# One adaLN transformer block on one core: an exp issued ahead of later softmaxes, one block's statistics on VectorE, the last rows in 384 and 128 columns, another issue order

## The chip, the core and the metric

The kernel runs on one core of a Trainium2 chip. The core has five engines that run side by side: TensorE (matmuls; PE in the profile, its weight loads PEld), VectorE (DVE), ScalarE (ACT), GpSimd (POOL) and SyncE (SP), which here only issues DMAs. Each engine works through its own list in the order in which the program issued it, and waits on semaphores for the others. The metric is the device time of one execution in microseconds (us); the median of several runs counts.

## The reference

```python
x = A_x                                                       # (1, 2048, 512), bfloat16
mod = (silu(c) @ w_mod).reshape(1, 6, 1, 512)                 # sa, ca, ga, sb, cb, gb
h = layernorm(x) * (1 + ca) + sa
x = x + ga * attention(h, wqkv, wo)
h = layernorm(x) * (1 + cb) + sb
x = x + gb * ((gelu(h @ w_gate) * (h @ w_up)) @ w_down)       # hidden width 1792
# attention: 32 heads of 16; position s attends to s, s-2, ..., s-14 (8 places):
#   softmax over the 8 logits q[s].k[s-2w] / 4, those before position 0 masked out
```

## The kernel before, in words

**Tiling.** The 2048 rows are worked in four groups of 512 rows (sg = 0 to 3), each of four blocks of 128 rows (c4 = 0 to 3). For each group the stages are: norm 1 (`ln1`, `norm`), transpose so that features lie on partitions (`transp`, `transp_ev`), the q, k and v projections (`qkv`, evicted by `qkv_ev`), logits, softmax, weighted sum, output projection (`x1_mm`) with the residual added (`x1_ev`, line 744), norm 2, the two up projections (`ffn_mm`, line 763), gelu and product (`ffn_act`, lines 796 and 803; `ffn_dve`, line 814), and the down projection (line 775) with the residual (line 821) and a store of each block of 128 rows (line 846).

**Attention without small matmuls.** VectorE multiplies q with the eight shifted views of k (`logits`, line 616, one instruction of 128x4096 for each of four slices j), and TensorE adds up each head's 16 products with a matrix of ones and zeros, 32 rows at a time, four at once (`logits_mm`, line 630, tile LTp in PSUM). The softmax (`soft`) takes the maximum (line 647), subtracts it (653), takes exp on ScalarE (658), sums (663), inverts (669) and scales (674). The weights go out to DRAM and come back spread over partitions (`pt_dma`: lines 681 and 688, tile PT). v goes out too and comes back as four loads (`vload`: 590 and 598, tile V). VectorE multiplies them (`pv`, line 700), and TensorE adds up over the eight places with the same ones (line 714, tile o_ps).

**Norms.** `norm` takes the statistics of a block on VectorE (line 394, then the aggregate in 400 and an added constant in 414); the blocks listed in the table `ACT_CH` get theirs on ScalarE, by a Copy and a Square pass that add up their output (`norm_act`, lines 377 and 383; the constant in 419). GpSimd raises to the power of -1/2 (line 425, tile rstd) for all four blocks of a group at once. VectorE then norms the blocks (line 434, tile xn). Group 3's norm 1 is transposed by a DMA (line 454), and ScalarE scales and shifts the result in place (line 486, tile hT).

**Table loads.** ScalarE works exp and gelu from different tables; where the next function needs the other one, the program has an ACT_TABLE_LOAD just ahead of the instruction. At the start the program issues a tiny exp into a scratch tile (line 325), so that exp's table is there early; for groups 2 and 3, whose softmax comes between gelus, there is none.

**What sets the order.** Every stage is a generator of operations (`Op`: an engine, a function that issues one or a few instructions, what must have been issued before, which slots of a pool it takes and gives back). `Issuer.run` goes through the table `ORDER`: each number says from which generator the next operation is taken. Since each engine runs in issue order, this table of 869 numbers is the schedule. The pools are small: four PSUM banks for the large matmuls (tag mm), two for attention (att), one pair for the logits (lg), four product tiles (prod), three each for gelu outputs and casts.

**DMAs.** All loads and stores but two go through SP's queue, in order; a DMA that waits for a semaphore holds up those behind it.

**The last rows.** The last block of group 3 is computed in two halves of 256 columns (line 786), each evicted (828) and stored (837) by itself.

Of the kernel before, what the change touches and what calls it, by code (L numbers as in the profile page):

```python
# [8 lines left out]
ACT = mybir.ActivationFunctionType  # L9
ALU = mybir.AluOpType  # L10
# [94 lines left out]
def kernel(  # L105
# [13 lines left out]
    nc = tc.nc  # L119
# [243 lines left out]
    ACT_CH = {"LN1.0": (3, 4), "LN1.1": (3, 4), "LN1.2": (2, 4), "LN1.3": (0, 4), "LN2.0": (0, 2), "LN2.1": (0, 4)}  # L363
# [274 lines left out]
    def soft(sg):  # L638
# [20 lines left out]
        yield Op("ACT", 0.97, f, after=[f"z.{sg}"], act="exp", fire=f"e.{sg}")  # L659
# [17 lines left out]
        yield Op("DVE", 1.14, f, give=[SL["lg"]], fire=f"p.{sg}")  # L677

# [75 lines left out]

    def ffn_mm(sg):
# [24 lines left out]
        if sg == NSG - 1:  # L780
            for ch in range(2):
                def f(ch=ch):
                    ps = T("mm", [P, D // 2], F32, "y_ps")
                    B["yl", ch] = ps
                    for ft in range(FT):
                        nc.tensor.matmul(ps[:], lhsT=B["hh", sg, ft][:, (CPS - 1) * P:],  # L786
                                         rhs=B["Wd", ft // 4][:, ft % 4, ch * 256:ch * 256 + 256],
                                         start=(ft == 0), stop=(ft == FT - 1))
                yield Op("PE", 1.53, f, take=[SL["mm"]], fire=f"yl.{ch}")
# [19 lines left out]
    def ffn_dve(sg):  # L809
# [13 lines left out]
        if sg == NSG - 1:  # L823
            for ch in range(2):
                def f(ch=ch):
                    ot = T("o", [P, D // 2], BF16, "ot")
                    B["otl", ch] = ot
                    nc.vector.tensor_tensor(out=ot[:], in0=B["yl", ch][:],
                                            in1=B["x", sg][:, CPS - 1, ch * 256:ch * 256 + 256], op=ALU.add)
                yield Op("DVE", 0.37, f, after=[f"yl.{ch}"], take=[SL["o"]], give=[SL["mm"]], fire=f"otl.{ch}")  # L830

    def stores(sg):
        if sg == NSG - 1:
            yield from stores_n(sg, CPS - 1)
            for ch in range(2):
                def f(ch=ch):
                    nc.sync.dma_start(out=out[0, S - P:S, ch * 256:ch * 256 + 256], in_=B["otl", ch][:])
                yield Op("SP", 0.4, f, after=[f"otl.{ch}"], give=[SL["o"]], fire=f"sto.l{ch}", lat=0.15)
# [20 lines left out]
    for sg in range(NSG):  # L859
        for n, g in (("sa1", lambda q: norm_act(lambda: B["x", q], x_ready(q), f"LN1.{q}")),  # L860
# [4 lines left out]
            pl.spawn(g(sg))  # L865
    with tc.manual_schedule():
        pl.run()
# [30 lines left out]
```

## Time and profile before

| | us |
|---|---|
| three runs | 237.60, 237.67, 239.79 |
| median | 237.67 |
| the profiled execution, its own time | 237.65 |
| its span, first to last instruction | 235.9 |
| TensorE busy | 230.1 (98%) |
| VectorE busy | 167.0 (71%) |
| ScalarE busy | 150.1 (64%) |
| GpSimd busy | 29.2 (12%) |
| granted TensorE clock | 1.000 |

In the lines of the timeline the columns are: start (us from the span's start), duration, engine, source line, operation, output tile<-inputs, shapes, count of merged instructions, and in brackets the idle time of the engine before it with what ended it. SPq is SP's queue, issuing a DMA. Lines of groups give busy time and mean ns of one after the bar, lines of DMA issues the KB of one and the median us from issue to landing.

### The profile page before, as it was taken

How to read it: one execution, taken by the hardware profiler on the slowest of the kernel's cores; microseconds unless marked ns; L12 is line 12 of the kernel's file. 1: busy time of each engine (PE TensorE's matmuls, PEld its weight loads, DVE VectorE, ACT ScalarE, POOL GpSimd, SP SyncE). 2: the span in 40 equal slices, each digit the busy share in tenths (PEclk: the TensorE clock that was granted, in tenths of full speed). 3: DMA queues.
4: the chain of work that ended last, by engine and by line, in shares of the span. 5: the costliest groups of instructions: out<-in, count | busy, mean ns of one | idle time of the engine just before them, and what ended most of it. 6: DMA issues, size and time to landing. Idle time of an engine off the chain costs nothing.

```text
span 235.9 us, 3647 instructions
## 1 busy us (share of the span) xinstructions
PE 230.1 (98%) x1382; PEld 107.7 (46%) x1382; DVE 167.0 (71%) x237; ACT 150.1 (64%) x284; POOL 29.2 (12%) x37
## 2 busy tenths in 40 slices
PE   7999999999999999999999999999999999999994
PEld 2755454434544444444443444444444444444444
DVE  4889998999998999969999988937622030423222
ACT  4899998696996758648556772652578531366400
POOL 3215205793100000200000010000100000000000
PEclk9999999999999999999999999999999999999999
DMA  6998775899667076052202833201040000100011
GB/s 218 385 306 272 260 235 149 195 382 408 279 186 195 0 250 253 0 114 74 61 0 61 307 90 69 67 0 44 22 92 1 0 22 0 47 0 22 0 44 47
DMA packets 30217, 30.42 MB, mean 129 GB/s; under 512 B 14712, under 2 KB 26104, under 8 KB 30200
## 3 DMA queue, kind: packets, MB, share of 16 engines
q1 hardware_dynamic: 29664, 29.67, 39.8%
q10 hardware_dynamic: 536, 0.53, 0.6%
q8 instruction: 11, 0.18, 0.3%
q14 instruction: 6, 0.05, 0.1%
HBM read 22.78 MB, written 5.31 MB: 119 GB/s over the span
## 4 chain that ended last, share of the span: by engine, by line
PE 75%; DVE 13%; DMA 4%; ACT 4%; issue 1%; POOL 1%; SPq 0%; ACTq 0%
PE u_ps L763 18%; PE g_ps L763 18%; PE y_ps L775 14%; PE qkv_ps L553 11%; PE x_ps L735 6%; DVE pq L616 5%; PE LTp L630 3%; PE o_ps L714 3%; DMA wm<-in_w_mod_dram 2%; DMA hT<-xn 2%; PE y_ps L786 1%; ACT hT L486 1%; DVE ssum L663 1%; DVE pv L700 1%; DVE e L674 1%
## 5 line engine op out<-in xcount | busy, mean ns | idle before, releaser
L763 PE MATMUL g_ps<-h,Wg 128*128 128x512 bf16 x224 | 57.2, 379 | 0.1
L763 PE MATMUL u_ps<-h,Wu 128*128 128x512 bf16 x224 | 57.2, 379 | 0.0
L814 DVE TENSOR_TENSOR hht<-gl,ub 128x512 bf16<-128x512 bf16 x56 | 22.9, 419 | 40.7 <-ACT ub L803 31.6
L796 ACT ACTIVATE gl<-g_ps 128x512 bf16<-128x512 f32 x56 | 33.6, 600 | 27.5 <-PE g_ps L763 25.9
L775 PE MATMUL y_ps<-Wd,hht 128*128 128x512 bf16 x210 | 47.0, 379 | 0.0
L803 ACT CAST ub<-u_ps 128x512 bf16<-128x512 f32 x56 | 32.8, 586 | 16.7 <-PE u_ps L763 16.5
L553 PE MATMUL qkv_ps<-hT,wqkv 128*128 128x512 bf16 x184 | 42.2, 380 | 0.2 <-ACT hT L486 0.2
L616 DVE TENSOR_TENSOR pq<-qT,kT 128x4096 bf16<-128x4096 bf16 x16 | 36.1, 2284 | 0.8 <-ACT kT L569 0.8
L700 DVE TENSOR_TENSOR pv<-PT,V 128x4096 bf16<-128x4096 bf16 x16 | 35.9, 2282 | 0.0
L763 PEld LDWEIGHTS <-Wg 128*128 128x128 bf16 x224 | 21.8, 98 | 27.1 <-issue 1.1
L763 PEld LDWEIGHTS <-Wu 128*128 128x128 bf16 x224 | 21.6, 98 | 27.2 <-issue 1.7
L775 PEld LDWEIGHTS <-hht 128*128 128x128 bf16 x210 | 20.4, 98 | 25.2 <-issue 0.8
L553 PEld LDWEIGHTS <-wqkv 128*128 128x128 bf16 x184 | 20.3, 114 | 18.8 <-issue 2.3
L425 POOL TENSOR_TENSOR rstd<-rstd,neghalf 128x4 f32<-128x4 f32 (+1 forms) x9 | 10.1, 1123 | 129.7 <-DVE rstd L414 70.0
L586 POOL COPY vh<-vT 128x64 bf16<-128x64 bf16 x3 | 15.9, 5284 | 7.9 <-ACT vT L571 7.9
L821 DVE TENSOR_TENSOR ot<-y_ps,x 128x512 bf16<-128x512 f32 x15 | 10.2, 685 | 7.5 <-PE y_ps L775 7.5
L735 PE MATMUL x_ps<-woP,oT 128*128 128x512 bf16 x64 | 15.5, 379 | 0.0
L744 DVE TENSOR_TENSOR x<-x_ps,x 128x512 bf16<-128x512 f32 x16 | 10.6, 682 | 5.4 <-PE x_ps L735 5.1
L394 DVE BATCH_NORM_STATS2 st<-x 128x6 f32<-128x512 bf16 x18 | 11.8, 680 | 2.5 <-DMA x<-in_A_x_dram 2.5
L377 ACT ACTIVATE gl<-x 128x512 bf16<-128x512 bf16 x14 | 9.1, 649 | 6.2 <-DVE x L744 4.5
L486 ACT ACTIVATE h<-h,modT,scl 128x512 bf16<-128x512 bf16 x12 | 9.0, 804 | 6.3 <-DMA h<-xn 6.3
L725 ACT CAST oT<-o_ps 128x512 bf16<-128x512 f32 x16 | 8.9, 583 | 4.5 <-PE o_ps L714 4.5
(76 smaller groups left out, 188.9 us busy)
## 6 DMA issues: line engine op xcount, KB each, us to landing
V<-vscr SPq DMA_DIRECT2D x16, 526.0 KB, 6.4
wm<-in_w_mod_dram SPq DMA_DIRECT2D x5, 512.0 KB, 5.6
vscr<-vT SPq DMA_DIRECT2D x4, 528.0 KB, 4.0
out_dram<-ot SPq DMA_DIRECT2D x15, 128.0 KB, 2.1
Wg<-in_B_w_gate_dram SPq DMA_DIRECT2D x1, 1792.0 KB
Wu<-in_B_w_up_dram SPq DMA_DIRECT2D x1, 1792.0 KB, 13.3
wqkv<-in_A_wqkv_dram SPq DMA_DIRECT2D x3, 512.0 KB, 7.3
x<-in_A_x_dram SPq DMA_DIRECT2D x3, 512.0 KB, 8.7
```

Source lines behind the costliest of these rows:

```text
L394: nc.vector.bn_stats(out=k["st", c4][:], in_=src()[:, c4, :])
L486: nc.scalar.activation(out=o, in_=B[key, dtp][:, :, dd, :] if pe else o, func=ACT.Identity, scale=sc(dt), bias=bi(dt))
L553: nc.tensor.matmul(ps[:], lhsT=wqkv[blk][:, dt, j::4], rhs=B["hT", sg][:, :, dt, :], start=(dt == 0), stop=(dt == DT - 1))
L586: yield Op("POOL", 0.2, lambda: nc.gpsimd.tensor_copy(out=vh[:], in_=B["vT", sg][:, :, SG:VR]), after=[f"qkv.{sg}.2.3"], fire=f"vh.{sg}")
L616: nc.vector.tensor_tensor(out=pq[:], in0=_ap(B["qT", sg][:, j, :], [[0, W], [1, SG]]), in1=_ap(kT[:, j, sg * SG + 2:sg * SG + 2 + SG], [[2 ...
L700: nc.vector.tensor_tensor(out=t[:], in0=_ap(B["PT", sg][:, 0, :], [[SG, 2], [0, 4], [1, SG]]), in1=_ap(v[:, j, 0, :], [[8, 2], [VR, 4], [1 ...
L735: nc.tensor.matmul(ps[:], lhsT=B["oT", sg][:, j, c4 * P:(c4 + 1) * P], rhs=woP[:, j, :], start=(j == 0), stop=(j == 3))
L763: nc.tensor.matmul(ps[:], lhsT=Wt[:, dt, ft * P:(ft + 1) * P], rhs=B["h2T", sg][:, :, dt, :], start=(dt == 0), stop=(dt == DT - 1))
L775: nc.tensor.matmul(ps[:], lhsT=B["hh", sg, ft][:, c4 * P:(c4 + 1) * P], rhs=B["Wd", ft // 4][:, ft % 4, :], start=(ft == 0), stop=(ft == F ...
L796: nc.scalar.activation(out=gl[:], in_=B["g", sg, ft][:], func=ACT.Gelu_apprx_tanh)
L803: nc.scalar.copy(out=ub[:], in_=B["u", sg, ft][:])
L814: nc.vector.tensor_tensor(out=hh[:], in0=B["gl", sg, ft][:], in1=B["ub", sg, ft][:], op=ALU.mult)
```

## The change

1. A new generator, `exp_table`, issues two tiny exps on ScalarE (4 columns, into the scratch tile), one for group 2 and one for group 3; each real exp of these groups must come after its own.
2. In `ACT_CH` block 0 of group 3's norm 1 leaves ScalarE's list, so that its statistics are taken on VectorE.
3. The last block's columns are split 384 and 128 instead of 256 and 256: matmuls, evictions and stores.
4. `ORDER` is another sequence throughout, with 872 numbers for 869 (one Copy and one Square less, two tiny exps more, three small VectorE operations more).

```diff
@@ -16,40 +16,40 @@
 NEG = -4.0e9
 
 ORDER = [
-    0, 10, 1, 2, 2, 10, 20, 10, 0, 20, 20, 20, 10, 20, 10, 10, 10, 1, 9, 21, 10, 10, 18, 2, 21, 10, 10, 21, 18,
...
+    0, 10, 1, 26, 2, 2, 10, 20, 10, 10, 10, 1, 10, 9, 10, 20, 10, 10, 9, 10, 20, 0, 10, 18, 2, 0, 2, 18, 9, 21,
...
 ]
 
 
@@ -360,7 +360,7 @@
             nc.vector.tensor_tensor(out=woP[:], in0=woP[:], in1=_ap(gB[:], [[0, 4], [1, D]]), op=ALU.mult)
         yield Op("DVE", 1.14, wos, after=["ga"] + [f"wo{i}" for i in range(4)], fire="woS")
 
-    ACT_CH = {"LN1.0": (3, 4), "LN1.1": (3, 4), "LN1.2": (2, 4), "LN1.3": (0, 4), "LN2.0": (0, 2), "LN2.1": (0, 4)}
+    ACT_CH = {"LN1.0": (3, 4), "LN1.1": (3, 4), "LN1.2": (2, 4), "LN1.3": (1, 4), "LN2.0": (0, 2), "LN2.1": (0, 4)}
     NS = {}
 
     def norm_tiles(ev):
@@ -656,7 +656,7 @@
 
         def f():
             nc.scalar.activation(out=B["z", sg][:], in_=B["z", sg][:], func=ACT.Exp, scale=DH ** -0.5)
-        yield Op("ACT", 0.97, f, after=[f"z.{sg}"], act="exp", fire=f"e.{sg}")
+        yield Op("ACT", 0.97, f, after=[f"z.{sg}"] + ([f"pre.{sg}"] if sg > 1 else []), act="exp", fire=f"e.{sg}")
 
         def f():
             B["ssum", sg] = smp["ssum"].tile([P, P], F32, name="ssum")
@@ -675,6 +675,11 @@
                                     in0=_ap(B["z", sg][:], [[4 * P, 2], [P, 4], [1, P]]),
                                     in1=_ap(B["rinv", sg][:], [[0, 2], [0, 4], [1, P]]), op=ALU.mult)
         yield Op("DVE", 1.14, f, give=[SL["lg"]], fire=f"p.{sg}")
+
+    def exp_table():
+        for sg in (2, 3):
+            yield Op("ACT", 0.15, lambda: nc.scalar.activation(out=junk[:], in_=neghalf[:], func=ACT.Exp), act="exp",
+                     fire=f"pre.{sg}")
 
     def pt_dma(sg):
         def f():
@@ -751,6 +756,8 @@
     def ln2_ev(sg):
         yield from transp_ev(("xn2", sg), ("h2T", sg), "h2", lambda d: scl[:, 4 + d:5 + d],
                              lambda d: modT[:, 4 + d:5 + d], f"LN2.{sg}", ["mod3", "mod4"])
+
+    LAST = ((0, 384), (384, 512))
 
     def ffn_mm(sg):
         h2 = [f"LN2.{sg}.h3"]
@@ -778,15 +785,14 @@
                 yield Op("PE", 1.51, f, after=dep, take=[SL["mm"]] if half == 0 else [],
                          give=[SL["hh"]] * 7 if c4 == CPS - 1 else [], fire=f"y.{sg}.{c4}.{half}")
         if sg == NSG - 1:
-            for ch in range(2):
-                def f(ch=ch):
-                    ps = T("mm", [P, D // 2], F32, "y_ps")
+            for ch, (a, b) in enumerate(LAST):
+                def f(ch=ch, a=a, b=b):
+                    ps = T("mm", [P, b - a], F32, "y_ps")
                     B["yl", ch] = ps
                     for ft in range(FT):
                         nc.tensor.matmul(ps[:], lhsT=B["hh", sg, ft][:, (CPS - 1) * P:],
-                                         rhs=B["Wd", ft // 4][:, ft % 4, ch * 256:ch * 256 + 256],
-                                         start=(ft == 0), stop=(ft == FT - 1))
-                yield Op("PE", 1.53, f, take=[SL["mm"]], fire=f"yl.{ch}")
+                                         rhs=B["Wd", ft // 4][:, ft % 4, a:b], start=(ft == 0), stop=(ft == FT - 1))
+                yield Op("PE", 3.06 * (b - a) / D, f, take=[SL["mm"]], fire=f"yl.{ch}")
 
     def ffn_act(sg):
         for ft in range(FT):
@@ -821,20 +827,19 @@
                 nc.vector.tensor_tensor(out=ot[:], in0=B["y", sg, c4][:], in1=B["x", sg][:, c4, :], op=ALU.add)
             yield Op("DVE", 0.605, f, after=[f"y.{sg}.{c4}.1"], take=[SL["o"]], give=[SL["mm"]], fire=f"ot.{sg}.{c4}")
         if sg == NSG - 1:
-            for ch in range(2):
-                def f(ch=ch):
-                    ot = T("o", [P, D // 2], BF16, "ot")
+            for ch, (a, b) in enumerate(LAST):
+                def f(ch=ch, a=a, b=b):
+                    ot = T("o", [P, b - a], BF16, "ot")
                     B["otl", ch] = ot
-                    nc.vector.tensor_tensor(out=ot[:], in0=B["yl", ch][:],
-                                            in1=B["x", sg][:, CPS - 1, ch * 256:ch * 256 + 256], op=ALU.add)
+                    nc.vector.tensor_tensor(out=ot[:], in0=B["yl", ch][:], in1=B["x", sg][:, CPS - 1, a:b], op=ALU.add)
                 yield Op("DVE", 0.37, f, after=[f"yl.{ch}"], take=[SL["o"]], give=[SL["mm"]], fire=f"otl.{ch}")
 
     def stores(sg):
         if sg == NSG - 1:
             yield from stores_n(sg, CPS - 1)
-            for ch in range(2):
-                def f(ch=ch):
-                    nc.sync.dma_start(out=out[0, S - P:S, ch * 256:ch * 256 + 256], in_=B["otl", ch][:])
+            for ch, (a, b) in enumerate(LAST):
+                def f(ch=ch, a=a, b=b):
+                    nc.sync.dma_start(out=out[0, S - P:S, a:b], in_=B["otl", ch][:])
                 yield Op("SP", 0.4, f, after=[f"otl.{ch}"], give=[SL["o"]], fire=f"sto.l{ch}", lat=0.15)
         else:
             yield from stores_n(sg, CPS)
@@ -863,6 +868,7 @@
                      ("x1", x1_ev), ("ln2", ln2), ("t2", lambda q: transp(("xn2", q), ("h2T", q), "h2", f"LN2.{q}")), ("h2", ln2_ev),
                      ("ffn", ffn_mm), ("act", ffn_act), ("hh", ffn_dve), ("st", stores)):
             pl.spawn(g(sg))
+    pl.spawn(exp_table())
     with tc.manual_schedule():
         pl.run()
```

The table's rows tell a reader nothing, so here is what three places of it look like on the engines, row for row in issue order (x2 stands for two in succession).

VectorE from group 0's first product (pq) to the first pv product. st, mv and rstd are a norm's statistics, xn its output, LTp, mx, ssum and e the softmax of group 0, woP a scaling of weights. Before:

```order
L616 TENSOR_TENSOR pq<-qT,kT 128x4096 x3
L394 BN_STATS st<-x 128x6 x2
L400 BN_AGGR mv<-st 128x2 x2
...
L674 TENSOR_TENSOR e<-LTp,rinv 128x2x4x128
L616 TENSOR_TENSOR pq<-qT,kT 128x4096 x2
L419 TENSOR_SCALAR rstd<-sums 128x4
L360 TENSOR_TENSOR woP<-woP,gB 128x2048
L434 TENSOR_SCALAR xn<-x,sums,rstd 128x512 x4
L700 TENSOR_TENSOR pv<-PT,V_577 128x4096 x4
```

Now, the same stretch:

```order
L394 BN_STATS st<-x 128x6
L616 TENSOR_TENSOR pq<-qT,kT 128x4096 x2
L400 BN_AGGR mv<-st 128x2
L394 BN_STATS st<-x 128x6
L400 BN_AGGR mv<-st 128x2
...
L419 TENSOR_SCALAR rstd<-sums 128x3
L674 TENSOR_TENSOR e<-LTp,rinv 128x2x4x128
L616 TENSOR_TENSOR pq<-qT,kT 128x4096
L434 TENSOR_SCALAR xn<-x,mv,rstd 128x512
L616 TENSOR_TENSOR pq<-qT,kT 128x4096
L434 TENSOR_SCALAR xn<-x,sums,rstd 128x512 x3
```

The statistics of group 2's norm moved ahead of group 0's last products, a third one (group 3's block 0) was added, and group 3's small add and normed blocks moved from behind group 1's two products and woP's scaling to places ahead of and between them; woP's scaling and the pv products follow.

ScalarE around group 2's exp and the gelus behind it (gl are gelus, ub casts, h the scaled norm 2 of group 1). Before:

```order
L803 CAST ub<-u_ps 128x512
L658 ACT_TABLE_LOAD
L658 ACTIVATE LTp<-LTp 128x1024
L486 ACTIVATE h_1523<-h_1523,modT,scl 128x4x128 x4
L796 ACT_TABLE_LOAD
L796 ACTIVATE gl<-g_ps 128x512
```

Now, and further on around the second tiny exp:

```order
L809 CAST ub<-u_ps 128x512
L681 ACT_TABLE_LOAD
L681 ACTIVATE junk<-neghalf 128x4
L658 ACTIVATE LTp<-LTp 128x1024
L486 ACTIVATE h_1506<-h_1506,modT,scl 128x4x128 x4
L802 ACT_TABLE_LOAD
...
L681 ACT_TABLE_LOAD
L681 ACTIVATE junk<-neghalf 128x4
L809 CAST ub<-u_ps 128x512
L802 ACT_TABLE_LOAD
L802 ACTIVATE gl<-g_ps 128x512
...
L658 ACT_TABLE_LOAD
```

Group 2's load moved ahead of the instruction that waits for VectorE. Group 3's tiny exp stands between the gelu and the cast of the fourth pair of group 1, with gelus behind it, so its table is loaded again at its own exp.

SP's queue ahead of group 1's pv products (V are v's loads, gscr and gB the last modulation row, escr and PT the softmax's weights). Before:

```order
L208 DMA Wu<-in_B_w_up_dram 128x4x1792
L598 DMA V_969<-vscr_109 128x1x2104
L223 DMA wm<-in_w_mod_dram 128x4x512
L598 DMA V_969<-vscr_109 128x1x2104 x3
L297 DMA gscr_115<-gR 4x128
L681 DMA escr_117<-e 128x1024
L243 DMA Wd_1151<-in_B_w_down_dram 128x4x512
L688 DMA PT<-escr_117 128x4x128 x2
```

Now:

```order
L598 DMA V_881<-vscr_109 128x1x2104
L304 DMA modc<-gscr_114 128x4x1
L598 DMA V_881<-vscr_109 128x1x2104
L297 DMA gscr_115<-gR 4x128
L598 DMA V_881<-vscr_109 128x1x2104
L686 DMA escr_117<-e 128x1024
L598 DMA V_881<-vscr_109 128x1x2104
L693 DMA PT<-escr_117 128x4x128 x2
```

The store of the last modulation row (gscr_115) moved ahead of the last two V loads; a load of down-projection weights moved behind PT.

66 rows, old and new, of the table ORDER are left out of this document.

## Prediction

> **What bounds the kernel now.** I read the head of the page first, then TensorE's timeline, then what VectorE and ScalarE were doing where TensorE paused. All times are microseconds.
>
> ```profile
> span 235.9 us, 3647 instructions
> PE 230.1 (98%) x1382; PEld 107.7 (46%) x1382; DVE 167.0 (71%) x237; ACT 150.1 (64%) x284; POOL 29.2 (12%) x37
> ```
>
> TensorE is busy 98% of the span, and the changed program gives it the same matmuls. So the question is only how much TensorE waits. A busy figure hides short pauses, because matmul ends are modelled; the start times tell more.
>
> ```profile
> 32.62 2.54 PE L553 MATMUL qkv_ps<-hT,wqkv 128*128 128x512 bf16 x11
> 35.43 0.62 PE L630 MATMUL LTp<-pq,Mph 128*32 128x512 bf16 x8 [0.27 <-DVE pq L616]
> 47.29 1.70 PE L553 MATMUL qkv_ps<-hT,wqkv 128*128 128x512 bf16 x7
> 49.18 0.38 PE L553 MATMUL qkv_ps<-hT,wqkv 128*128 128x512 bf16 x1 [0.19 <-ACT hT L486]
> 49.65 1.15 PE L714 MATMUL o_ps<-pv,Mph 128*32 128x512 bf16 x16
> ...
> 110.83 1.03 PE L763 MATMUL u_ps<-h,Wu 128*128 128x512 bf16 x4
> 111.99 1.02 PE L763 MATMUL g_ps<-h,Wg 128*128 128x512 bf16 x4
> ...
> 126.19 0.60 PE L714 MATMUL o_ps<-pv,Mph 128*32 128x512 bf16 x8
> 127.14 0.61 PE L714 MATMUL o_ps<-pv,Mph 128*32 128x512 bf16 x8 [0.35 <-DVE pv L700]
> ...
> 132.01 1.03 PE L735 MATMUL x_ps<-woP,oT 128*128 128x512 bf16 x4
> 133.03 1.02 PE L763 MATMUL g_ps<-h,Wg 128*128 128x512 bf16 x4
> ```
>
> The seven matmuls at 47.29 last 1.70, of which 0.38 is the last one's own length (the row of one at 49.18): six steps in 1.32, so a full matmul costs 0.216 and four cost 0.86. What starts later than that is a stall. 35.43 comes 2.81 after 32.62, where eleven matmuls (2.38) and a switch to the 32-row form (taken as 0.1) need 2.48: 0.33. At 49.18 seven matmuls (1.51) explain 48.80: 0.38. At 49.65, 0.47 after one matmul (0.22) and a switch: 0.16. At 111.99, 1.16 for 0.86: 0.30. At 127.14, 0.95 where eight of the 32-row form, four at a time, take 0.44: 0.51. At 133.03, 1.02 for 0.86: 0.16. Together 1.84 in 236. After 133 TensorE runs without a pause to the end, so no saving there can reach the end except in the last rows. The releasers are VectorE's products and evictions, and for 49.18 the transpose of group 3's norm. So until 133 VectorE and TensorE are tied together, and each tie is worth tenths.
>
> **The change: group 3's statistics.** One block's mean and variance go from ScalarE to VectorE. VectorE pays a statistics instruction (0.60 from start to start), an aggregate (0.12) and one more small add (0.13): 0.85, placed ahead of group 1's first product. ScalarE loses a Copy and a Square pass.
>
> ```profile
> 23.81 1.28 DVE L394 BATCH_NORM_STATS2 st<-x 128x6 f32<-128x512 bf16 x2
> ...
> 29.70 1.22 DVE L663 TENSOR_REDUCE ssum<-LTp 128x128 f32<-128x1024 f32 x1 [0.37 <-ACT LTp L658]
> ...
> 33.09 4.48 DVE L616 TENSOR_TENSOR pq<-qT,kT 128x4096 bf16<-128x4096 bf16 x2
> 37.82 1.23 DVE L360 TENSOR_TENSOR woP<-woP,gB 128x2048 bf16<-128x2048 bf16 x1
> 39.95 1.38 DVE L434 TENSOR_SCALAR xn<-x,sums,rstd 128x512 bf16<-128x512 bf16 x4 [0.90 <-POOL rstd L425]
> 41.25 2.28 DVE L700 TENSOR_TENSOR pv<-PT,V 128x4096 bf16<-128x4096 bf16 x1
> ```
>
> The softmax chain of group 0 starts 0.7 later and the 0.37 wait for exp disappears behind the other work, so the first product of group 1 starts at 33.09 + 0.85 - 0.37 = 33.6 instead of 33.09, and TensorE's stall at 35.4 grows from 0.33 to about 0.9: a loss of 0.5. It comes back: group 3's reciprocal root now runs ahead of that product, on an idle GpSimd, so that the 0.90 of waiting at 39.95 goes. From 33.09 to 41.25 VectorE takes 8.16 before and 7.26 without the 0.90, so pv starts at 33.6 + 7.26 = 40.9, which is 0.4 earlier. The normed rows (1.38 of work that used to end at 41.3) now come ahead of woP's scaling and end 1.2 + 0.4 sooner, and their transpose with them, so the stall of 0.38 at 49.18 goes too. TensorE, 0.5 to 0.6 late at 36.0, gives up 0.38 + 0.16 there, and one switch less between matmul forms (group 1's second logits matmul now stands inside group 0's o_ps stretch) saves 0.2; it reaches the last o_ps of group 0 some 0.3 earlier. Taken: **-0.3**; bounds 0 (the loss just paid back) and -0.4 (all of VectorE's lead). If GpSimd misses its window ahead of the product, it is held:
>
> ```profile
> 26.91 1.01 POOL L425 TENSOR_TENSOR rstd<-rstd,neghalf 128x4 f32<-128x4 f32 x1 [2.62 <-DVE rstd L419]
> 37.86 2.05 POOL L425 TENSOR_TENSOR rstd<-rstd,neghalf 128x4 f32<-128x4 f32 x1 [9.95 <-DVE rstd L419]
> 42.82 11.82 POOL L586 COPY vh<-vT 128x64 bf16<-128x64 bf16 x1 [1.73 <-ACT vT L571]
> ```
>
> The same operation takes twice as long under VectorE's woP scaling, and a small copy waited out six products. Held by one product, the norm would come 0.6 to 1 late, which takes the -0.3 away.
>
> **The tiny exps.** Group 2's exp waits for a table.
>
> ```profile
> 102.73 1.28 ACT L658 ACT_TABLE_LOAD   x1 [4.45 <-DVE LTp L653]
> 105.07 1.23 DVE L663 TENSOR_REDUCE ssum<-LTp 128x128 f32<-128x1024 f32 x1 [1.82 <-ACT LTp L658]
> ```
>
> The load stood behind the wait for VectorE; the tiny exp waits for nothing, so its load falls into the 4.45 of idle ScalarE. That takes 1.3 off the 1.82 that VectorE waits, and all of VectorE's work down to the pv products of group 2 moves up: the evictions that end the stall at 111.99 and the product that ends the one at 127.14 come 1.3 earlier (**-0.30** and **-0.51**). One eviction is put behind another product, 2.2 more, but in the new order the bank that it frees is asked for two groups of four matmuls later, 1.7, and the 1.3 comes off as well. Bounds: both stalls stay (0), or both go (-0.81); 1.3 against 0.30 and 0.51 leaves room, so I take the whole.
>
> For group 3 the order is different. The tiny exp is issued four gelus early, so that the gelu table and then the exp table are loaded again: two loads more than before.
>
> ```profile
> 122.63 1.03 PE L763 MATMUL g_ps<-h,Wg 128*128 128x512 bf16 x4
> ```
>
> ```profile
> 119.43 0.59 ACT L803 CAST ub<-u_ps 128x512 bf16<-128x512 f32 x1 [2.33 <-PE u_ps L763]
> 120.24 0.60 ACT L796 ACTIVATE gl<-g_ps 128x512 bf16<-128x512 f32 x1 [0.22 <-PE g_ps L763]
> ...
> 128.41 1.28 ACT L658 ACT_TABLE_LOAD   x1
> 131.09 1.28 ACT L796 ACT_TABLE_LOAD   x1
> 132.38 0.60 ACT L796 ACTIVATE gl<-g_ps 128x512 bf16<-128x512 f32 x1
> ```
>
> The first extra load (1.28) and the tiny exp (0.2) fit in the 2.33 of idle ahead of 119.43; the second, behind that cast, delays the next gelu from 120.24 to 121.2, done by 121.8, and the matmuls that take its bank start at 122.63. So hidden with 0.8 to spare: cost 0; uncovered it would be 1.28. In the old order the gelu at 132.38, ending at 132.98, released the matmul at 133.03; now it is ahead of the exp and its two loads: **-0.16**.
>
> The Trainium skill ("ScalarE: Activation LUTs", What ACT_TABLE_LOAD costs) adds a drain of about 1.38 to each load, 2.66 for a switch. Here the next ACTIVATE starts 1.29 after the load's start (131.09 to 132.38), so the trace shows no such drain.
>
> **The last rows** in 384 and 128 columns.
>
> ```profile
> 17.74 0.61 PE L448 MATMUL hTp<-ident,xn 128*128 128x128 bf16 x8
> ...
> 229.93 0.69 DVE L821 TENSOR_TENSOR ot<-y_ps,x 128x512 bf16<-128x512 f32 x1 [2.33 <-PE y_ps L775]
> 232.99 0.42 DVE L828 TENSOR_TENSOR ot<-y_ps,x 128x256 bf16<-128x256 f32 x1 [1.10 <-PE y_ps L786]
> ```
>
> TensorE's total stays: narrow matmuls run at their width (eight of 128 columns, each with its own weights, are through in 0.61). The last eviction shrinks from 0.42 to about 0.29 (0.69 at 512 and 0.42 at 256 give 0.27 for 256 columns). The 384-column eviction ends before it is needed. So **-0.13**, if the store lands as fast.
>
> ```profile
> PT<-escr SPq DMA_DIRECT2D x8, 128.0 KB, 2.4
> out_dram<-ot SPq DMA_DIRECT2D x2, 64.0 KB, 1.5
> ```
>
> Stores of 64 KB land in 1.5; the nearest with rows of 128 columns is the PT load, 2.4 for 128 KB. Bounds of the tail: -0.13 and +0.8; I take the first, as it is the same kind of store. The Trainium skill ("DMA: Bandwidth & Descriptors", Specifications) asks for 512 bytes and more per transfer and names a read-modify-write below; the new rows have 256. By that rule the tail would lose (rival D); no row here shows such a store.
>
> **Sum.** The profiled execution took 237.65 (span 235.9 and 1.75 around it), 0.02 under the median of 237.67. 237.65 - 0.3 - 0.30 - 0.51 - 0.16 - 0.13 = 236.25: **236.2**.
>
> **Rivals.** *A, the gain stays off TensorE's path* (chance 0.27): the group 3 norm is held by a product (term 0), and the 0.51 and 0.16 turn into waits at other places. Left are 0.30 and the tail: 237.2. For it: every tie above is worth under 0.6, and VectorE carries 0.85 more. Against it: the 1.3 taken off at 105 is more than the 0.85.
>
> *B, the SP queue* (0.12), the case that ends slower. A store of the last modulation row, which goes at 63.37, now stands ahead of two of group 1's V loads and of the softmax store; before, the V loads left early.
>
> ```profile
> 51.41 2.71 SPq L598 DMA_DIRECT2D V<-vscr  x3
> 63.37 0.55 SPq L297 DMA_DIRECT2D gscr<-gR  x1
> 65.72 0.34 SPq L681 DMA_DIRECT2D escr<-e  x1
> 72.48 4.49 DVE L700 TENSOR_TENSOR pv<-PT,V 128x4096 bf16<-128x4096 bf16 x2
> V<-vscr SPq DMA_DIRECT2D x16, 526.0 KB, 6.4
> ```
>
> If the last V load, issued near 65.6, takes its 6.4 and PT lands 2.4 after it, pv starts at 74.4, not at the 72.2 that the 0.3 gained would give: 2.2 late, with TensorE waiting on it, 238.4. It decides once PT lands after 72.2. Against it: 6.4 was measured behind the large weights, which are through by then, and in the old order a load of 512 KB stood at the same place.
>
> *C, the table switches are not hidden* (0.05): if a switch keeps ScalarE for twice the 1.29, the exp's runs from 117.1 (where the idle 2.33 begins) to 119.7, the tiny exp to 119.9, the cast to 120.4, the gelu's switch to 123.0, and the gelu ends at 123.6, 1.0 after its bank is wanted: 237.2. The row at 132.38 speaks against it. The skill's 2.66 is about that price.
>
> *D, the narrow store lands late* (0.05): 2.4 as PT, instead of 1.5: 237.1. The skill's rule on 512 bytes would have it so.
>
> **How the numbers follow.** Forecast 0.45, A 0.27, B 0.12, C 0.05, D 0.05; 0.06 for what I haven't seen, half of it either way. A measurement of this kernel tells about 1% (2.4) from no change. The stalls are 1.84, so faster by over 1% needs all of them and more: 0.06, half from the forecast's edge and half unseen. Slower by over 1% (over 240.0) is B with PT landing 4 late, 0.05 of its 0.12, and half the unseen: 0.08. Within: 0.86. Range: all stalls and the tail gone give 235.7, and I allow 0.4 for waits under 0.1 that I did not list; B gives 238.4: 235.3 to 238.5.
>
> **What would show it.** Right: nine table loads; the sum at group 2 waiting under 0.7; TensorE's four-matmul steps at 111 and the o_ps pair at 126 without a gap; a stall at 35.4 of 0.6 to 1.1; hT's transpose landing near 44.3. Wrong: a gap of over 1 at 72 to 77 on VectorE (B), a gelu that ends a TensorE wait at 119 to 125 (C), GpSimd's root at 32 to 37 taking 2 or more (A).

## The result, and the profile after

The changed kernel takes 236.13 (median of 20 runs, 235.58 to 238.19) against 237.72 for the kernel before (20 runs, 237.34 to 240.54): a ratio of 0.9929, 95% interval 0.9906 to 0.9952, so 0.7% faster and within 1%. The prediction was 236.2 in a range of 235.3 to 238.5. The profiled execution took 235.66, near the short end of its runs. All times are microseconds.

The head of its page, then TensorE's timeline in two stretches:

```profile
span 233.9 us, 3653 instructions
PE 229.1 (98%) x1382; PEld 106.9 (46%) x1382; DVE 168.2 (72%) x240; ACT 152.5 (65%) x284; POOL 24.3 (10%) x37
```

```profile
24.34 0.62 PE L630 MATMUL LTp<-pq,Mph 128*32 128x512 bf16 x8
25.12 0.61 PE L630 MATMUL LTp<-pq,Mph 128*32 128x512 bf16 x8 [0.16 <-DVE pq L616]
...
33.61 1.89 PE L553 MATMUL qkv_ps<-hT,wqkv 128*128 128x512 bf16 x8
35.60 0.62 PE L630 MATMUL LTp<-pq,Mph 128*32 128x512 bf16 x8
```

```profile
110.09 1.03 PE L770 MATMUL u_ps<-h,Wu 128*128 128x512 bf16 x4
110.95 1.03 PE L770 MATMUL g_ps<-h,Wg 128*128 128x512 bf16 x4
111.82 1.03 PE L770 MATMUL u_ps<-h,Wu 128*128 128x512 bf16 x4
...
125.09 1.05 PE L719 MATMUL o_ps<-pv,Mph 128*32 128x512 bf16 x16
126.07 1.04 PE L770 MATMUL u_ps<-h,Wu 128*128 128x512 bf16 x4
...
130.40 1.89 PE L740 MATMUL x_ps<-woP,oT 128*128 128x512 bf16 x8
132.12 1.03 PE L770 MATMUL g_ps<-h,Wg 128*128 128x512 bf16 x4
```

TensorE's busy share is 98% as before; the gain shows in the start times. From 110.09 four matmuls follow every 0.86 or 0.87: the pauses of 0.30, 0.51 and 0.16 that stood at 112, 127 and 133 are gone. Early on, two short pauses are left where the kernel before had 0.33 and, at 49, 0.38 and 0.16. The pair at 25.12 starts 0.78 after eight of the 32-row form (0.44): 0.34 late. At 35.60, 1.99 after eight matmuls (1.73) and a switch (0.09), it is 0.17. Group 3's norm is out of the way: ScalarE scales its transposed rows (hT) at 44.63, early enough that TensorE's sixteen matmuls at 45.45 run through (49.02 less 45.45 is 3.57, of which sixteen take 3.46 and a switch 0.09):

```profile
44.63 2.94 ACT L486 ACTIVATE hT<-hT,modT,scl 128x512 bf16<-128x512 bf16 x4
```

```profile
45.45 3.64 PE L553 MATMUL qkv_ps<-hT,wqkv 128*128 128x512 bf16 x16
49.02 1.05 PE L719 MATMUL o_ps<-pv,Mph 128*32 128x512 bf16 x16
```

**A ruler for the experiments.** In profiled executions of one program the start of the run varies and the rest does not. This is the first full projection matmul of the changed kernel (an execution of 235.66):

```profile
10.80 7.07 PE L553 MATMUL qkv_ps<-hT,wqkv 128*128 128x512 bf16 x32
```

235.66 - 10.80 is 224.86; the same kernel without its tiny exps, in an execution of 236.64, starts that matmul at 11.77, which leaves 224.87. Six profiled executions of the changed kernel and near variants gave 224.86 or 224.87 while their first matmul moved from 10.73 to 14.55. In three experiments (a_noexp2, a_noexp3, b_exp2) TensorE's granted clock from 10 to 15 was only 0.73, 0.57 and 0.50 of full and that matmul came late (14.07 to 15.48); ratios here, and the medians of the experiments, leave out runs that such a clock made long. I call the time from that matmul on "the rest"; differences of 0.1 show in it, while the intervals of the ratios are 0.5 to 0.9 wide to either side, so that a_act and b_order cannot be told from the kernel before by their runs alone, and b_exp2 only just.

The rest still holds the time around the span, 1.71 or 1.72 in most of these executions and 1.79 or 1.80 in four (a_same2, a_best, b_exp2, b_split). That is the 0.1 by which two of the eight changed kernels differ. Where 0.1 matters, I compare from the first projection matmul to the first matmul of the last rows. The kernel before shows how steady that is: it takes 229.73 - 10.84 = 218.89, and b_split, which is the same program up to there, 229.90 - 11.03 = 218.87.

| kernel | profiled execution | first L553 | the rest | ratio to before, 95% |
|---|---|---|---|---|
| before | 237.65 | 10.84 | 226.81 | |
| changed | 235.66 | 10.80 | 224.86 | 0.9929 (0.9906 to 0.9952) |
| changed, again (a_same) | 235.77 | 10.91 | 224.86 | 0.9925 (0.9892 to 0.9958) |
| changed, a third time (a_same2) | 236.36 | 11.40 | 224.96 | 0.9915 (0.9884 to 0.9946) |
| without group 2's tiny exp (a_noexp2) | 238.93 | 14.07 | 224.86 | 0.9933 (0.9895 to 0.9972) |
| without group 3's (a_noexp3) | 239.41 | 14.55 | 224.86 | 0.9931 (0.9892 to 0.9971) |
| without both (a_noexp) | 236.64 | 11.77 | 224.87 | 0.9923 (0.9891 to 0.9954) |
| V loads moved (a_sp) | 235.60 | 10.73 | 224.87 | 0.9889 (0.9853 to 0.9925) |
| without both, V loads moved (a_best) | 236.09 | 11.14 | 224.95 | 0.9921 (0.9891 to 0.9952) |
| changed, statistics back (a_act) | 238.13 | 11.28 | 226.85 | 0.9975 (0.9942 to 1.0008) |
| before, one tiny exp (b_exp2) | 241.32 | 15.48 | 225.84 | 0.9962 (0.9924 to 1.0000) |
| before, two moves (b_order) | 236.87 | 11.12 | 225.75 | 0.9974 (0.9943 to 1.0005) |
| before, statistics alone (b_stat) | 237.72 | 11.03 | 226.69 | 0.9965 (0.9937 to 0.9993) |
| before, last rows alone (b_split) | 237.70 | 11.03 | 226.67 | one execution |

### The profile page after: what moved, and what is told of

Read it like the earlier page. It is cut to its first block, busy times and chain, and to the rows that moved or that the text cites. A ratio compares the mean times of both kernels' runs of the same rounds, so it can differ in the third digit from the quotient of the medians.

```text
span 233.9 us, 3653 instructions
## 1 busy us (share of the span) xinstructions
PE 229.1 (98%) x1382; PEld 106.9 (46%) x1382; DVE 168.2 (72%) x240; ACT 152.5 (65%) x284; POOL 24.3 (10%) x37
## 4 chain that ended last, share of the span: by engine, by line
PE 84%; DVE 9%; DMA 3%; ACT 1%; SPq 1%; issue 0%
PE g_ps L770 21%; PE u_ps L770 21%; PE y_ps L782 19%; PE qkv_ps L553 9%; PE x_ps L740 6%; DVE pq L616 5%; PE o_ps L719 3%; DMA x<-in_A_x_dram 3%; PE LTp L630 2%; PE y_ps L793 1%; DVE xn L434 1%; DVE st L394 1%; ACT qT L567 1%; DVE e L674 1%; DVE LTp L653 1%; DVE mx L647 1%
## 5 line engine op out<-in xcount | busy, mean ns | idle before, releaser
L802 ACT ACTIVATE gl<-g_ps 128x512 bf16<-128x512 f32 x56 | 33.6, 600 | 18.4 <-PE g_ps L770 16.9
L553 PE MATMUL qkv_ps<-hT,wqkv 128*128 128x512 bf16 x184 | 42.2, 380 | 0.0
L553 PEld LDWEIGHTS <-wqkv 128*128 128x128 bf16 x184 | 20.1, 114 | 18.5 <-issue 2.3
L425 POOL TENSOR_TENSOR rstd<-rstd,neghalf 128x4 f32<-128x4 f32 (+1 forms) x9 | 8.7, 971 | 124.4 <-DVE rstd L414 74.7
L394 DVE BATCH_NORM_STATS2 st<-x 128x6 f32<-128x512 bf16 x19 | 12.6, 680 | 2.7 <-DMA x<-in_A_x_dram 2.6
L586 POOL COPY vh<-vT 128x64 bf16<-128x64 bf16 x3 | 11.7, 3899 | 14.5 <-ACT vT L571 14.5
L377 ACT ACTIVATE gl<-x 128x512 bf16<-128x512 bf16 x13 | 8.3, 645 | 4.7 <-DVE x L749 3.0
```

What stands on the lines that cost most here:

```text
L394: nc.vector.bn_stats(out=k["st", c4][:], in_=src()[:, c4, :])
L553: nc.tensor.matmul(ps[:], lhsT=wqkv[blk][:, dt, j::4], rhs=B["hT", sg][:, :, dt, :], start=(dt == 0), stop=(dt == DT - 1))
L586: yield Op("POOL", 0.2, lambda: nc.gpsimd.tensor_copy(out=vh[:], in_=B["vT", sg][:, :, SG:VR]), after=[f"qkv.{sg}.2.3"], fire=f"vh.{sg}")
L802: nc.scalar.activation(out=gl[:], in_=B["g", sg, ft][:], func=ACT.Gelu_apprx_tanh)
```

## The experiments

The prediction's theory: the statistics cost VectorE 0.5 and are paid back, and the tiny exp of group 2 is what moves its table load. The rivals below say that ScalarE was the tight engine early on, or that the issue order itself did the work.

### Who freed the table load

The changed kernel without group 2's tiny exp, without group 3's, and without both (the last also takes the generator out):

```diff
     def exp_table():
-        for sg in (2, 3):
+        for sg in (3,):        # a_noexp2; (2,) in a_noexp3
...
 ORDER: the number 122 once less (a_noexp: twice less)
```

> The changed kernel without the tiny exp of group 2. Theory 1, the prediction's: the table load goes back behind VectorE's subtraction, the sum waits 1.3 longer and TensorE's pauses near 110 and 126 come back: 0.5 to 0.8 slower than the changed kernel. Theory 2, the new order has brought VectorE 0.75 earlier into this stretch and has slack of its own (waits of 0.39 and 0.31 on VectorE at 111.8 and 116.0), so that it would have hidden the load without the tiny exp: 0 to 0.3 slower.

> The changed kernel without the tiny exp of group 3, so with two table loads fewer. Theory 1, the prediction's: the loads lie in ScalarE's idle time, no change within 0.1, seven loads. Theory 2: the load between cast and gelu at 118.9 delays the gelu to 120.2 and what follows, so without it 0.2 to 0.5 faster.

> The changed kernel without both tiny exps. In the run without group 2's, the table load of the real exp stood ahead of its wait for VectorE: in the new order that exp waits for VectorE alone, where it waited for VectorE and TensorE before, and then the load sat between the two waits. Theory 1, the new order itself freed the load: the same time as the changed kernel within 0.2, the sum at group 2 waiting 0.5, seven table loads. Theory 2, the prediction's, the tiny exp freed it: 0.5 to 0.8 slower, the sum waiting 1.8.

And the kernel before with only the tiny exp of group 2, issued just ahead of the real one:

```diff
+    def exp_table():
+        yield Op("ACT", 0.15, lambda: nc.scalar.activation(out=junk[:], in_=neghalf[:], func=ACT.Exp), act="exp",
+                 fire="pre.2")
...
 ORDER: + 122 ahead of group 2's exp
```

> The kernel before, with the tiny exp of group 2 alone put ahead of the real one, and nothing else. Theory 1, the prediction's: the wait of 1.82 for exp falls to about 0.5, and the pauses of 0.30 at 112 and 0.51 at 127 go (perhaps the 0.16 at 133 too): 0.8 to 1.0 faster than the kernel before. Theory 2, the pauses are set by the order and by buffers, not by the load: under 0.3 faster, with the pauses still there.

The first matmul of the last rows, in the kernel before and with the tiny exp:

```profile
229.73 3.22 PE L786 MATMUL y_ps<-Wd,hht 128*128 128x256 bf16 x28
```

```profile
233.33 3.22 PE L790 MATMUL y_ps<-Wd,hht 128*128 128x256 bf16 x28
```

Counted from their first projection matmuls (10.84 and 15.48) these are 218.89 and 217.85: the tiny exp alone takes 1.04 off the kernel before (the rest shows 0.97, as this execution has 0.08 more around its span). The three pauses (0.30, 0.51, 0.16) are gone from TensorE's timeline. But taking it out of the changed kernel costs nothing: all three rests are 224.86 or 224.87, where the prediction's theory had 0.5 to 0.8. The sum of group 2 in the changed kernel, then ScalarE and VectorE of the kernel without both tiny exps, each from its timeline:

```profile
102.38 1.23 DVE L663 TENSOR_REDUCE ssum<-LTp 128x128 f32<-128x1024 f32 x1 [0.48 <-ACT LTp L658]
```

```profile
98.92 1.28 ACT L658 ACT_TABLE_LOAD   x1
102.31 1.01 ACT L658 ACTIVATE LTp<-LTp 128x1024 f32<-128x1024 f32 x1 [2.11 <-DVE LTp L653]
```

```profile
103.35 1.22 DVE L663 TENSOR_REDUCE ssum<-LTp 128x128 f32<-128x1024 f32 x1 [0.48 <-ACT LTp L658]
```

The load belongs to the real exp (L658), no tiny exp is there, and yet it runs ahead of the wait for VectorE; the sum waits 0.48 as in the changed kernel, not 1.82. In the kernel before it stood behind that wait. The view of line 658 there shows why:

```profile
L658 ACT ACT_TABLE_LOAD  x2: 1283/1283/1283, 102.7 to 128.4; - x2
L658 ACTq EVENT_SEMAPHORE  x1: 17/17/17, 102.7 to 102.7; - x1
```

There is one separate semaphore instruction, at 102.7, group 2's exp. The issued program has the same at that place (first the kernel before, then the changed one without tiny exps):

```
L658 ACT_TABLE_LOAD [waits DVE_49]
L658 ACTIVATE LTp<-LTp 128x1024 [waits PE_49]

L658 ACT_TABLE_LOAD
L658 ACTIVATE LTp<-LTp 128x1024 [waits DVE_49]
```

In the kernel before, that exp waits for two engines, VectorE's subtraction and TensorE's logits (DVE_49 and PE_49 are their semaphores); one wait is put ahead of the load and the other on the exp. In the new order ScalarE has already waited for a later matmul, the wait for TensorE falls away, the one wait left sits on the exp, and the load goes ahead. To test this without a tiny exp and without the rest of the new order, two moves in the kernel before:

```diff
 ORDER, VectorE: group 2's last product (pq) ahead of group 3's first
 ORDER, TensorE:
-L763 u_ps (14th), L775 y_ps x7, L630 LTp x16
+L630 LTp x16, L763 u_ps (14th), L775 y_ps x7
```

> The kernel before without any tiny exp, with two moves: VectorE's last product of group 2 goes ahead of group 3's first, and TensorE's sixteen logits matmuls of group 2 go ahead of the last up projection, whose eviction ScalarE waits for before the exp. So the exp's wait for TensorE falls away as in the new order, and one wait is left. Theory 1, the second wait is what put the table load behind the wait for VectorE: the load starts in ScalarE's idle time, the sum waits 0.5, the pauses at 112 and 127 go, 0.6 to 1.0 faster than the kernel before, as with the tiny exp. Theory 2, only an exp that is issued earlier moves the load: no change within 0.2, the sum waiting 1.8.

```profile
98.33 0.59 ACT L803 CAST ub<-u_ps 128x512 bf16<-128x512 f32 x1 [0.27 <-PE u_ps L763]
98.94 1.28 ACT L658 ACT_TABLE_LOAD   x1
102.95 1.01 ACT L658 ACTIVATE LTp<-LTp 128x1024 f32<-128x1024 f32 x1 [2.73 <-DVE LTp L653]
```

```profile
103.99 1.23 DVE L663 TENSOR_REDUCE ssum<-LTp 128x128 f32<-128x1024 f32 x1 [0.48 <-ACT LTp L658]
```

```profile
111.08 1.03 PE L763 MATMUL u_ps<-h,Wu 128*128 128x512 bf16 x4
111.95 1.03 PE L763 MATMUL g_ps<-h,Wg 128*128 128x512 bf16 x4
...
126.08 1.05 PE L714 MATMUL o_ps<-pv,Mph 128*32 128x512 bf16 x16
127.06 1.04 PE L763 MATMUL u_ps<-h,Wu 128*128 128x512 bf16 x4
```

The load starts right behind the cast (98.94), the sum waits 0.48, the pauses at 112 and 127 are gone, and the rest is 225.75: 1.06 less than before, with no tiny exp. (The 1.06 also holds whatever the two moves do by themselves; the tiny exp, without them, was worth 1.04.) So the second wait is shown to be what kept the load back; in the changed kernel the order frees the load, and both tiny exps change nothing.

### The statistics

The kernel before with the statistics move alone, and the changed kernel with it undone:

```diff
-"LN1.3": (0, 4)          # b_stat, from the kernel before
+"LN1.3": (1, 4)
 ORDER: one Copy and one Square out; L394 behind group 2's two, L400 ahead of L653, L414 ahead of L669
...
-"LN1.3": (1, 4)          # a_act, from the changed kernel
+"LN1.3": (0, 4)
 ORDER: L394, L400 and L414 of group 3 out; a Copy ahead of its three, a Square ahead of its three
```

> The kernel before with the statistics of group 3's block 0 on VectorE and no other move: the statistics instruction right behind the two of group 2, its two small operations between operations of the softmax of group 0 that depend on each other, the power of -1/2 still behind group 1's second product. Theory 1, ScalarE was the tight engine and the small operations cost VectorE nothing: between 0.3 faster and 0.1 slower. Theory 2, VectorE pays 0.85 less the 0.37 of waiting, and TensorE's pause at 35.4 grows from 0.33 to 0.8: 0.3 to 0.5 slower.

> The changed kernel with block 0 of group 3's norm 1 back on ScalarE (a Copy and a Square more there, a statistics instruction, an aggregate and an add fewer on VectorE), the rest of the new order as it is. Theory 1, ScalarE was the tight engine: it has no idle time between 15.8 and 36.9 in the changed kernel, so the two passes (1.3 together) push its evictions of group 2's norm and the matmuls at 36.15 back: 0.6 to 1.3 slower than the changed kernel, TensorE's pause ahead of 36.15 grown by that. Theory 2, VectorE was the tight engine, as the prediction had it with its loss of 0.5: the first product of group 1 starts 0.4 to 0.7 earlier than 33.27, and the kernel is 0.3 to 0.5 faster than the changed one.

The reciprocal in the kernel before (the sum ahead of it stands in the prediction, at 29.70), then VectorE of the kernel before with the statistics alone:

```profile
30.96 0.95 DVE L669 RECIPROCAL rinv<-ssum 128x128 f32<-128x128 f32 x1
```

```profile
29.97 1.22 DVE L663 TENSOR_REDUCE ssum<-LTp 128x128 f32<-128x1024 f32 x1
31.10 0.14 DVE L414 TENSOR_SCALAR rstd<-mv 128x1 f32<-128x1 f32 x1
31.22 0.95 DVE L669 RECIPROCAL rinv<-ssum 128x128 f32<-128x128 f32 x1
32.20 1.23 DVE L674 TENSOR_TENSOR e<-LTp,rinv 128x1024 bf16<-128x1024 f32 x1
33.34 4.49 DVE L616 TENSOR_TENSOR pq<-qT,kT 128x4096 bf16<-128x4096 bf16 x2
```

The first matmul of this execution is 0.19 later than before (11.03 and 10.84), so the product's 33.34 stands for 33.15 against 33.09: it lost 0.06, where theory 2 had 0.85 less 0.37, and the idle time ahead of TensorE's matmuls at 35.4 grew by 0.14 (0.27 to 0.41), where theory 2 had it grow by 0.5. The rest is 0.12 shorter. A reason can be read in the steps. From the sum to the reciprocal, which needs the sum, it is 1.25 here with an add in between, and was 1.26 (29.70 to 30.96) without one: the dependent step waits for the result anyway, and the small add, which starts 0.09 before the sum's end (31.10, end 31.19), fits in.

With the statistics back on ScalarE the changed kernel loses 1.99 (224.86 to 226.85), more than theory 1's 0.6 to 1.3. TensorE and VectorE of that run:

```profile
28.45 0.41 PE L343 MATMUL gR_ps<-wm,scB 128*32 128x128 bf16 x16
30.13 1.89 PE L553 MATMUL qkv_ps<-hT,wqkv 128*128 128x512 bf16 x8 [1.27 <-ACT vT L571]
```

```profile
74.29 4.49 DVE L705 TENSOR_TENSOR pv<-PT,V 128x4096 bf16<-128x4096 bf16 x2 [0.73 <-DMA PT<-escr]
```

TensorE waits 1.27 for a projection's eviction that now stands behind the two passes: ScalarE was the tight engine, ahead of 30.13 and not at 36.15 as expected. The last row is rival B's place: PT lands (at 74.19) too late for VectorE, which waits 0.73. TensorE's start times put 1.26 of the 1.99 ahead of 77, and the rest at 78.84, 83.57 and 93.85, behind VectorE's products. That the store on SP's queue made PT late here was not tested.

### SP's queue

```diff
 ORDER, SP's queue:
-V (2nd), gscr (last modulation row), V (3rd), escr, V (4th), PT
+V (2nd), V (3rd), V (4th), gscr, escr, PT
```

> The changed kernel with two of group 1's V loads moved back ahead of the store of the last modulation row on SP's queue. In the changed kernel PT of group 1 landed at 71.63, 0.11 before the first pv product started at 71.74. Theory 1, the queue costs nothing yet: the same time within 0.2, PT landing 0.5 to 1 earlier, the product at the same place. Theory 2, the prediction's rival B in small: PT landing late is what makes some runs of the changed kernel 0.5 to 1.5 longer than its fastest, and without it the median is 0.3 to 0.5 faster and the spread smaller.

> The changed kernel without both tiny exps and with the two V loads of group 1 ahead of the store on SP's queue. Theory 1: neither is on TensorE's path, so the time is that of the changed kernel within 0.2, PT of group 1 landing near 69.7 where it was 71.7. Theory 2, late landings of PT lengthen some runs of the changed kernel: the median 0.3 to 0.5 under that of the changed kernel in this call, and the spread smaller.

> The changed kernel itself once more, beside the others of this call on the same chip: about 1.6 faster than the kernel before. Theory 1 and theory 2 expect the same of it; it is what the other three are compared with.

> The changed kernel once more, on the chip of this call: 1.5 to 1.6 faster than the kernel before by both theories; it is there for the comparison with the kernel without tiny exps and with the V loads moved.

SP's queue in the timeline and the DMA issues (median us to landing at the end), of the changed kernel, then of the one with the V loads moved:

```profile
67.81 0.92 SPq L693 DMA_DIRECT2D PT<-escr  x2
```

```profile
PT<-escr SPq DMA_DIRECT2D x2, 128.0 KB, 3.4
```

```profile
66.92 0.92 SPq L693 DMA_DIRECT2D PT<-escr  x2
```

```profile
PT<-escr SPq DMA_DIRECT2D x2, 128.0 KB, 2.3
```

PT is issued 0.89 earlier and lands in 2.3, not 3.4: 69.7 where it was 71.63. But the first pv product starts at 71.67 after 71.74, because VectorE is only then free; the rest is the same (224.87; on another chip 224.95 beside 224.96). So rival B was there, 0.11 from deciding. The medians of these runs (235.84 and 236.47 on one chip, 236.61 and 236.35 on the other, the moved loads first) point both ways; that late landings lengthen some runs is not shown. In the rest, no version beat the changed kernel.

### The last rows

The kernel before with `LAST = ((0, 384), (384, 512))` and the three loops over it:

> The kernel before with its last rows in 384 and 128 columns, and nothing else; a look at its last 6. Theory 1, the prediction's: the last eviction takes 0.29 where it took 0.42, and the last store lands as fast as before, so the span from TensorE's last matmul to the end shrinks by 0.13 from 2.95 less 0.42. Theory 2, the prediction's rival D: a store of rows of 128 columns takes as long as the PT load, and that stretch grows by 0.8.

```profile
233.16 0.29 DVE L829 TENSOR_TENSOR ot<-y_ps,x 128x128 bf16<-128x128 f32 x1 [0.22 <-PE y_ps L788]
```

The eviction takes 0.29 for 0.42, and from TensorE's last matmul to the end it is 2.78 for 2.98. From its end to the end of the span it is 2.45, and 2.52 before: the narrow store is not late but 0.07 quicker. Rival D falls. The Trainium skill ("DMA: Bandwidth & Descriptors", Specifications) puts a read-modify-write on transfers under 512 bytes; with rows of 256 this store shows no price for it, though it also moves half the bytes.

## Why the prediction was right, and where it was not

The sum was made against the profiled execution and came to 236.25; that execution took 235.66, a gain of 1.99 and not 1.40. The median, 236.13, lies 0.47 above it; between profiled executions it is the start that varies, but the other runs left no trace. That 236.2 lies within 0.1 of the median is therefore luck: terms that were 0.6 too small met runs that were 0.5 longer than the profiled one. TensorE's lost time (start to start, beyond the matmuls' own lengths), counted from the first projection matmul, splits the rest:

| stretch | predicted | measured |
|---|---|---|
| up to 100 (group 3's statistics, early chain) | -0.3 | -0.70 |
| 100 to 134 | -0.97 | -1.04 |
| from TensorE's last matmul to the end | -0.13 | -0.22 |

**The loss of 0.5 at 35.4: wrong.** The step that failed is "starts at 33.09 + 0.85 - 0.37 = 33.6". It started at 33.27. VectorE in the changed kernel, to be laid beside the rows of before from 29.70 to 33.09:

```profile
29.89 1.22 DVE L663 TENSOR_REDUCE ssum<-LTp 128x128 f32<-128x1024 f32 x1
31.02 0.14 DVE L414 TENSOR_SCALAR rstd<-mv 128x1 f32<-128x1 f32 x1
31.14 0.95 DVE L669 RECIPROCAL rinv<-ssum 128x128 f32<-128x128 f32 x1
32.01 0.10 DVE L419 TENSOR_SCALAR rstd<-sums 128x3 f32<-128x3 f32 x1
32.13 1.23 DVE L674 TENSOR_TENSOR e<-LTp,rinv 128x1024 bf16<-128x1024 f32 x1
33.27 2.28 DVE L616 TENSOR_TENSOR pq<-qT,kT 128x4096 bf16<-128x4096 bf16 x1
```

From sum to product it is 3.38 with two adds in between, and was 3.39 with none. The new add, which I priced at 0.13, costs nothing between dependent steps, and neither does the one that moved up. That leaves 0.60 + 0.12 - 0.37 = 0.35 of my sum, but the sum of the softmax starts only 0.19 later (29.89 for 29.70); what saved the other 0.16 is open, as the order ahead of it changed too. The independent add starts 0.09 before the sum has ended (31.02, end 31.11); the reciprocal, when it followed directly, started 0.04 after the end. By the Trainium skill ("Perfetto Trace Analysis", DVE / Act Engine Instruction (TENSOR_ADD, Activation, etc)) the next instruction may begin to fetch its data when the one ahead has finished executing, while the end that the profiler reports is the acknowledgement of the write, with the semaphore's update. The 0.09 and the 0.04 agree with it, if the reciprocal waits for that update. I had taken durations, where an instruction's place decides its price.

So the pause at 35.4, which I had growing from 0.33 to 0.9, is 0.17 instead; a new one of 0.34 stands at 25.12, a loss of 0.18 in all. VectorE's lead came out larger too: the pv products start at 40.10, not at 40.9. The 0.38 and 0.16 went as forecast, and a third pause of 0.1, inside the sixteen matmuls at 49.65, that I hadn't listed went too: 0.64, less the 0.18, is a gain of 0.46. Another 0.24 up to 100 is spread over several places, matmul form switches among them (I had 0.2); no experiment separates them.

**ScalarE's relief: missing from the sum.** I listed the Copy and the Square as removed and gave them no value. In the old order the whole move is worth 0.12; in the new order, undoing it costs 1.99, with a wait of 0.73 for PT among its causes. So the new order needs the move, and neither figure is the price of the move by itself.

**The tiny exp of group 2: about the right size, wrong cause.** In the kernel before, the tiny exp does what I said, and somewhat more: I had 0.81 for it (0.30 and 0.51), and it is worth 1.04. The 0.16 at 133 is among that, with no gelu moved; I had given it to the gelu's new place ahead of the exp and its loads. In the changed kernel the order had already freed the load, so that the gain from 100 to 134 is the order's and the tiny exp's part in it is nothing. The rows that could have told me stood in the prediction: of two loads for L658, the one at 102.73 followed a wait of 4.45 and the one at 128.41 followed none, though both belong to an exp that waits for VectorE. I took the first as the rule.

**The tiny exp of group 3: right.** ScalarE of the changed kernel around it:

```profile
116.09 1.28 ACT L681 ACT_TABLE_LOAD   x1
117.38 0.21 ACT L681 ACTIVATE junk<-neghalf 128x4 f32<-128x4 f32 x1
118.34 0.59 ACT L809 CAST ub<-u_ps 128x512 bf16<-128x512 f32 x1 [0.75 <-PE u_ps L770]
118.94 1.28 ACT L802 ACT_TABLE_LOAD   x1
120.23 0.60 ACT L802 ACTIVATE gl<-g_ps 128x512 bf16<-128x512 f32 x1
```

There are nine loads, 1.29 from a load's start to its user, and the two extra ones lie in idle time: without this exp the rest is the same. Rival C falls.

**Group 3's root and the tail: right.** GpSimd's root (rival A's place) was not held:

```profile
32.20 1.01 POOL L425 TENSOR_TENSOR rstd<-rstd,neghalf 128x4 f32<-128x4 f32 x1 [1.63 <-DVE rstd L419]
```

It took 1.01, not 2, ending 0.06 before the product began. In the tail, 0.13 is the eviction and the rest the quicker store.

## What to carry to other kernels

Before a table load is moved by a dummy call, look at the waits of the instruction that needs it: as here, with one wait the load runs ahead of it, with two it can stand between them, and an order in which the second is already fulfilled is as good as the dummy. Price a small instruction by its place: between two dependent steps it can be free. And where runs differ in their start, compare profiled executions from the first large matmul on, before believing medians that differ by a few tenths.

## What the runs showed that I had not expected

The rest of a run repeats to 0.1 (224.86 to 224.96 in eight executions) while its first matmul there moves by almost 4 (10.73 to 14.55); and with two small adds put between its dependent steps a chain on VectorE took 3.38, where it had taken 3.39.
